# A 32x64 split of the DFT in a fused convolution and MLP kernel: row tiles, column tiles, larger transposes and a new order of work

## The chip, the cores and the metric

The kernel runs on one core of a Trainium2 chip. The metric is the device time of one execution in microseconds (us), less being better. The kernel before took 305.59 us, the median of three runs (304.36 to 305.82). A run is in the "fast" or the "slow" state ("slow" here: over 1.5% above the fastest run of the same kernel), or "unknown" when the kernel ran only once. Verdicts below use fast runs.

Names of engines: PE is TensorE (matrix multiplications), PEld its weight loads, DVE is VectorE, ACT is ScalarE, POOL is GpSimd, SP is SyncE, which here issues all the DMAs. "SPq" is SyncE's queue of instructions. An eviction is the copy of a matmul result out of PSUM, the memory that TensorE writes to. "kv" is the product of the filtered k and v; w1 to w4 are the weight matrices of the MLP (mlp1 is the product with w1); "gin" is what step 4 reads.

## The reference, cut to what matters

```python
def reference(A_q, A_k, A_v, A_shift_k, A_ssm_k, A_ssm_D, B_x, B_w1, ..., gate_w):
    # S = 2048 positions, D = 640 channels, F = 1536
    x = A_q
    g = sigmoid((x * gate_w).sum(-1, keepdims=True))
    # a: 4-tap causal filter of k, times v, then a causal convolution of length S
    kv = causal_filter(A_k, A_shift_k) * A_v
    y  = irfft(rfft(kv, 2*S) * rfft(A_ssm_k, 2*S))[:S] + kv * A_ssm_D
    a  = x * y
    # b: an MLP whose first half shifts four channel groups along the sequence by 1, -1, 2, -2
    h  = gelu(layernorm(x) @ w1)
    x1 = x + shifted(h) @ w2
    b  = x1 + gelu(layernorm(x1) @ w3) @ w4
    return g * a + (1 - g) * b
```

(The long convolution and the shift are condensed here into named helpers.) In both kernels the Fourier transform of length 4096 is done by matrix multiplications: step 1 transforms over the part of the position that lies on the 128 partitions, step 2 over the rest, then comes the product with the transformed filter, and steps 3 and 4 go back. Between the steps the data pass through DRAM.

The parts that the change and the argument touch:

```python
# position s = 16*t2 + t1: partition t2 (128 of them), t1 along the free dimension
q_rows = A_q.rearrange("b (t2 t1) d -> (b t2) t1 d", t1=NT)      # k_rows, v_rows, o_rows alike

def load_x(c):                                   # x is A_q; 4 of these, 640 KB each
    SP.dma_start(out=X[:, 4*c:4*c+4, :], in_=q_rows[:, 4*c:4*c+4, :])

def kv_load(c):
    ...
    SP.dma_start(out=K[:, r:r+n, :], in_=k_src(0, P, t0, n))      # outermost dimension: 128 rows
    SP.dma_start(out=st["KV"][...], in_=v_rows[:, KC*c:KC*c+KC, :])

def step1(name, hf, c, scr, ev):                 # whole array, 128 rows by 128 columns, two halves hf
    ...
            PE.matmul(ps[:, b*512:(b+1)*512], lhsT=F1[:, hf*P:(hf+1)*P], rhs=src[:, o:o+512], ...)
    ...                                          # all evictions of steps 1, 2 and 3 on ScalarE

def h_dma(c):                                    # five small DMA transposes for each quarter of h
    for f in range(4):
        SP.dma_start_transpose(out=st["HT"][:, f, 4*c:4*c+4, HPAD:HPAD+P], in_=hr[:, f]...)
    SP.dma_start_transpose(out=st["HM0"][...], in_=hr[:, 4]...)

def step4(t1, last):                             # two matmuls accumulate into the same 128 rows
    ...
    if t1 % 2 == 0:
        SP.dma_start(out=st["q2"][:], in_=q_rows[:, t1:t1+2, :])
    ...
        SP.dma_start(out=o_rows[:, t1, :], in_=ot[:])
```

## Time and profile before

| | before |
|---|---|
| time, median (range, runs) | 305.59 us (304.36 to 305.82, 3) |
| profiled span, mean granted TensorE clock | 302.3 us, 0.941 |
| busy: PE, DVE, ACT, POOL | 242.2, 176.9, 179.1, 28.3 us |
| last step-3 matmul | 255.7 us |

The first view is part 2 of the page of the kernel before: the span in 40 slices of 7.6 us. Each digit of PE and DMA is the busy share in tenths (DMA: mean over the core's 16 DMA engines), PEclk is the clock granted to TensorE, and the last row is the rate of the DMAs.

```profile
PE   2058858364639888999999999999999999995585
PEclk9999998975968999999999999999999999999559
DMA  6999979585699299958975458554975021775511
GB/s 201 242 259 401 206 202 314 96 236 170 157 283 400 59 269 280 359 205 225 321 288 173 129 193 194 183 173 128 413 242 174 3 87 43 245 278 175 175 43 43
```

TensorE has gaps in the first third and is full after that until the tail. The DMAs are busy in the first third, at 200 to 400 GB/s.

The second view is the kernel before cut into five stretches: for each one its length, then the busy us (and instructions) of PE, PEld, DVE, ACT and POOL, the granted clock, the DMA share and the rate in GB/s.

```profile
core 0: us, PE busy (x) PEld busy (x) DVE busy (x) ACT busy (x) POOL busy (x), PEclk, DMA share, GB/s
0.00:18.40 18.40, 2.83 (x10) 1.37 (x11) 14.13 (x68) 11.44 (x23) 4.56 (x11) 1.00 0.88 223
18.40:66.00 47.60, 34.94 (x240) 19.94 (x240) 37.08 (x89) 33.15 (x68) 5.78 (x4) 0.93 0.91 249
66.00:120.00 54.00, 36.01 (x200) 17.03 (x200) 44.03 (x97) 28.44 (x51) 3.53 (x3) 0.87 0.77 228
120.00:256.00 136.00, 134.04 (x796) 66.04 (x796) 49.59 (x42) 101.44 (x141) 14.45 (x13) 1.00 0.59 196
256.00:302.30 46.30, 34.34 (x191) 16.83 (x189) 32.02 (x50) 4.67 (x6) 0.00 (x0) 0.84 0.48 163
```

From 120 to 256 us TensorE works 134 of 136 us: that stretch is bound by it. The DMA share of the first two stretches is 0.88 and 0.91, so the DMAs are nearly full there too. (Later this view prints shares slightly above 1; read that as full.)

The third view is part 6 of the page, the DMA issues that the change renames: how many, KB of each, and the median us from issue to landing.

```profile
X<-in_A_q_dram SPq DMA_DIRECT2D x4, 640.0 KB, 7.4
KV<-in_A_v_dram SPq DMA_DIRECT2D x8, 320.0 KB, 4.5
q<-in_A_q_dram SPq DMA_DIRECT2D x8, 320.0 KB, 3.1
out_dram<-ot SPq DMA_DIRECT2D x16, 160.0 KB, 1.8
```

On SyncE's queue in the kernel before, the 20 transposes of h (16 to HT, 4 to HM0) take a median of 1.26 us each, and the first starts at 32.9 us.

### The profile page before, as it was taken

Reading aid. Unit: us, or ns where it says so; the run is one execution under the profiler, and the core shown is the slowest. Engines: PE = TensorE matmul, PEld = TensorE weight load, DVE = VectorE, ACT = ScalarE, POOL = GpSimd, SP = SyncE. Lnnn points to the kernel's source line nnn. Section 1 sums busy time; section 2 is a strip of 40 time slices with the busy share of each in tenths; the row PEclk is TensorE's granted clock in tenths of the full one; section 3 lists DMA queues with packets and bytes.
Section 4 is the critical chain, followed back from the end, with each engine's and each line's share of the span. In section 5 each row is a group of like instructions: output and inputs, shape, how many; then the busy total and the mean of one; then the engine's idle time right before and its main releaser. Section 6 shows DMA issues by size and latency. Waiting matters only on the chain.

```text
span 302.3 us, 3944 instructions
## 1 busy us (share of the span) xinstructions
PE 242.2 (80%) x1434; PEld 121.2 (40%) x1434; DVE 176.9 (58%) x344; ACT 179.1 (59%) x284; POOL 28.3 (9%) x31
## 2 busy tenths in 40 slices
PE   2058858364639888999999999999999999995585
PEld 1024535231205444444454445444445454453232
DVE  8767969927899876501125234462343724099983
ACT  1999867242626666997868886469793676400000
POOL 6011302000000211990000000000000000000000
PEclk9999998975968999999999999999999999999559
DMA  6999979585699299958975458554975021775511
GB/s 201 242 259 401 206 202 314 96 236 170 157 283 400 59 269 280 359 205 225 321 288 173 129 193 194 183 173 128 413 242 174 3 87 43 245 278 175 175 43 43
DMA packets 60307, 62.50 MB, mean 207 GB/s; under 512 B 34304, under 2 KB 51457, under 8 KB 60288
## 3 DMA queue, kind: packets, MB, share of 16 engines
q1 hardware_dynamic: 60288, 62.25, 67.2%
q8 instruction: 11, 0.18, 0.2%
q14 instruction: 8, 0.07, 0.1%
HBM read 35.55 MB, written 18.35 MB: 178 GB/s over the span
## 4 chain that ended last, share of the span: by engine, by line
PE 30%; DVE 22%; ACT 13%; SPq 7%; DMA 7%; issue 6%; POOL 1%; ACTq 0%; DVEq 0%; POOLq 0%
PE ps L604 9%; PE ps L596 8%; ACT xs L348 6%; SPq L516 5%; PE ps L321 3%; DVE hs L359 3%; DVE p L358 3%; DVE p L357 3%; PE ps L370 3%; DVE X L558 3%; ACT gs L374 3%; DVE ot L625 2%; ACT stg L323 2%; PE ps L372 2%; PE ps L346 2%
## 5 line engine op out<-in xcount | busy, mean ns | idle before, releaser
L604 PE MATMUL ps<-W,gt 128*128 128x512 bf16 (+1 forms) x384 | 62.5, 306 | 0.8 <-DVE ot L607 0.8
L596 PE MATMUL ps<-x1t,W 128*128 128x512 bf16 x240 | 59.0, 379 | 0.0
L323 ACT CAST stg<-ps 128x1024 bf16<-128x1024 f32 x40 | 38.4, 1020 | 20.5 <-PE ps L321 10.4
L509 PE MATMUL psm<-WA,xt 128*128 128x512 bf16 (+1 forms) x160 | 30.0, 348 | 20.3 <-DVE WA L455 10.2
L604 PEld LDWEIGHTS <-gt 128*128 128x128 bf16 x384 | 30.2, 99 | 24.8 <-issue 3.7
L610 DVE TENSOR_TENSOR X<-ps,X 128x640 bf16<-128x640 f32 x12 | 9.9, 823 | 47.9 <-PE ps L604 47.9
L596 PEld LDWEIGHTS <-W 128*128 128x128 bf16 x240 | 22.3, 97 | 25.2
L357 DVE TENSOR_TENSOR p<-xs,hs 64x2560 bf16<-64x2560 bf16 x8 | 11.9, 1487 | 33.2 <-ACT xs L348 33.2
L374 ACT CAST gs<-ps 128x640 bf16<-128x640 f32 x32 | 20.6, 695 | 16.7 <-PE ps L372 14.5
L597 ACT ACTIVATE gt<-ps 128x1024 bf16<-128x1024 f32 x24 | 24.6, 1027 | 8.0 <-PE ps L596 7.7
L509 PEld LDWEIGHTS <-xt 128*128 128x128 bf16 x160 | 14.9, 111 | 32.0 <-issue 18.5
L346 PE MATMUL ps<-ax,TB 128*128 128x512 bf16 (+1 forms) x128 | 26.2, 298 | 0.3
L554 PE MATMUL psw<-WA,HT 128*128 128x512 bf16 (+1 forms) x128 | 22.4, 306 | 4.6 <-DVE X L558 3.6
L348 ACT CAST xs<-ps 128x640 bf16<-128x640 f32 x32 | 20.2, 696 | 9.0 <-PE ps L346 8.9
L321 PE MATMUL ps<-HT,F 128*128 128x512 bf16 x40 | 13.4, 441 | 13.9 <-ACT stg L323 7.2
L348 ACT CAST hs<-ps 128x640 bf16<-128x640 f32 x32 | 20.3, 696 | 0.1
L464 POOL TENSOR_TENSOR rs<-ve,EXPO 128x4 f32<-128x4 f32 x8 | 10.3, 1290 | 106.7 <-DVE ve L572 70.3
L437 DVE TENSOR_TENSOR acc<-acc,tmp 128x1280 bf16<-128x1280 bf16 x24 | 19.7, 823 | 0.5
L432 DVE TENSOR_TENSOR tmp<-K,cj 128x1280 bf16<-128x1280 bf16 (+1 forms) x25 | 19.8, 794 | 0.4
L510 ACT ACTIVATE hr<-psm,rs 128x640 bf16<-128x640 f32 x16 | 12.6, 807 | 12.4 <-DMA HM<-hr 5.9
L616 PE MATMUL ps<-gin,F 128*128 128x512 bf16 (+1 forms) x64 | 13.4, 347 | 7.4 <-DVE gq L622 6.7
L622 DVE TENSOR_TENSOR gq<-ps,gq 128x640 bf16<-128x640 f32 x16 | 12.6, 825 | 11.0 <-PE ps L616 11.0
(99 smaller groups left out, 309.0 us busy)
## 6 DMA issues: line engine op xcount, KB each, us to landing
S_h<-stg SPq DMA_DIRECT2D x10, 512.0 KB, 4.1
ax<-S_h SPq DMA_DIRECT2D x8, 640.0 KB, 4.2
S_x<-stg SPq DMA_DIRECT2D x10, 512.0 KB, 3.0
ax<-S_x SPq DMA_DIRECT2D x8, 640.0 KB, 4.7
S_g<-gs SPq DMA_DIRECT2D x16, 320.0 KB, 2.3
gin<-S_g SPq DMA_DIRECT2D x8, 640.0 KB, 7.8
W<-in_B_w_dram SPq DMA_DIRECT2D x2, 1920.0 KB, 9.3
X<-in_A_q_dram SPq DMA_DIRECT2D x4, 640.0 KB, 7.4
```

The costliest lines, as they stand in the source:

```text
L321: PE.matmul(ps[:, b * 512:(b + 1) * 512], lhsT=F1[:, hf * P:(hf + 1) * P], rhs=src[:, o:o + 512], start=True, stop=True)
L323: A.copy(out=stg[:, u * 1024:(u + 1) * 1024], in_=ps[:])
L346: PE.matmul(ps[:, o:o + w], lhsT=st["T2"][:, g, :], rhs=ax[:, i, o:o + w], start=True, stop=True)
L348: A.copy(out=dst[:, i, :], in_=ps[:])
L357: V.tensor_tensor(out=p2[0:64], in0=x[0:64], in1=h[64:128], op=ALU.mult)
L374: A.copy(out=gs[:, i % 2, :], in_=ps[:])
L432: V.tensor_tensor(out=dst[:, i:i + n, :], in0=K[:, r:r + n, :], in1=cj[:, j:j + 1, :].to_broadcast([P, n, D]), op=ALU.mult)
L509: PE.matmul(ps[:, o:o + w], lhsT=xt[:, i, k, :], rhs=W1X[:, k, o:o + w], start=(k == 0), stop=(k == DC - 1))
L554: PE.matmul(ps[:, o:o + w], lhsT=h_tile(f, t1), rhs=W2P[:, f, o:o + w], start=(f == 0), stop=(f == 4))
L596: PE.matmul(ps[:, u, :].rearrange("p (a b) -> p a b", a=4), lhsT=st["W3"][:, k, f * P:(f + 1) * P], rhs=xt[:, :, k, :], start=(k == 0), st ...
L597: A.activation(out=gt[:, 2 * (fp % 2):2 * (fp % 2) + 2, :], in_=ps[:], func=ACT.Gelu_apprx_tanh)
L604: PE.matmul(ps[:, o:o + w], lhsT=st["gt", c, f // 4][:, f % 4, i * P:(i + 1) * P], rhs=st["W4"][:, f, o:o + w], start=(f == 0), stop=(f == ...
```

## The change

The intent: with only 64 positions on each half of the partitions, the step-1 matmul needs 64 rows of the array and the step-4 matmul fills 64 columns, so two can run side by side. The position becomes s = 32*t2 + 16*r + t1, and partition 64*r + t2 holds the pair (r, t2). Beside that, 20 small transposes of h become 4 large ones, the shifts are done by copies, part of the evictions goes from ScalarE to VectorE, scaling goes to GpSimd, and the order of all the work is written out as a fixed list.

```diff
-    q_rows = A_q.rearrange("b (t2 t1) d -> (b t2) t1 d", t1=NT)      # v_rows, o_rows alike
+    q_rows = A_q.rearrange("b (t2 r t1) d -> r (b t2) t1 d", r=2, t1=NT)
     def load_x(c):
-        SP.dma_start(out=X[:, 4 * c:4 * c + 4, :], in_=q_rows[:, 4 * c:4 * c + 4, :])
+        SP.dma_start(out=X[:, 4 * c:4 * c + 4, :], in_=q_rows[:, :, 4 * c:4 * c + 4, :])
     # kv_load: K (v alike)
-            SP.dma_start(out=K[:, r:r + n, :], in_=k_src(0, P, t0, n))
+            SP.dma_start(out=K[:, r:r + n, :], in_=bass.AP(..., ap=[[NT * D, 2], [32 * D, H], [D, n], [1, D]]))
     # step 1: two row tiles
-                PE.matmul(ps[:, b * 512:(b + 1) * 512], lhsT=F1[:, hf * P:(hf + 1) * P], rhs=src[:, o:o + 512], ...)
+                PE.matmul(ps[:, r, :], lhsT=F1[H * r:H * r + H, :], rhs=src[H * r:H * r + H, o:o + 512], ...)
     # step 4: two column tiles
-                PE.matmul(ps[:, o:o + w], lhsT=F4[:, hf, :], rhs=st["gin", hf][...], start=(hf == 0), stop=(hf == 1))
+                PE.matmul(ps[H * r:H * r + H, o:o + w1], lhsT=F4[:], rhs=g[:, r, ...], start=True, stop=True)
     # h: one transpose for each quarter
+        SP.dma_start_transpose(out=st["HT"][:, 4 * c:4 * c + 4]..., in_=hr[:]...)
     # q for the end: four loads through a ring of two buffers shared with other tiles; store of one tile
+        q2 = ring.tile([P, 4, D], BF16, name="q2", tag="row", bufs=2)
+        SP.dma_start(out=q2[:], in_=q_rows[:, :, 4 * c:4 * c + 4, :])
+            SP.dma_start(out=o_rows[:, :, t1, :], in_=X1[:, t1, :])
     # order: a list of names; the letters are the engines of the evictions
+        "... step2.h.0.VAVA scale_x1.2.V w4.2 step2.x.0.VAAV table.2 w3.1.0 step2.h.1.AVVA ... "
     (cut: tables, shifts by copy, gating, the rest of the order)
```

## The prediction

> **What bounds the kernel now.** Busy times by stretch show four regimes. From 0 to 66 us TensorE is busy 38 us; from 66 to 120, 36 of 54; from 120 to 256, 134 of 136 at full clock, so that stretch is TensorE-bound; from 256 to 302, 34 of 46. Only the first 120 us and the tail have slack to give back. In the first, the chain of waits runs from 52 to 82 us mostly over SyncE issuing transposes (20 small ones of h at 1.26 us each, plus four of x at 3.2 to 7.6) and then over the VectorE work for kv and w2. In the tail (timeline) VectorE does 0.82 + 0.89 + 0.39 us per step-4 tile while TensorE waits for it, and then 48 w4 matmuls run alone for 9 us.
>
> **Costed changes.**
> 1. Steps 1 and 4 keep their matmul counts (80 and 64) but pair them on disjoint halves of the array. At the 0.216 us spacing of 512-column matmuls seen here, step 1 takes 17 us and step 4 about 8.6. If pairs overlap, 8.6 and 4.3 us of TensorE go. The Trainium skill, "TensorEngine Tiling (Array Packing)", Key Properties, says tiles work in parallel but a mode switch drains the array; step 1 is interleaved with full-array matmuls, so I count half its gain. The transposes of the SSM kernel double to 160 (0.07 us each here: up to +5 us). Net TensorE: −5 to −8 us; step 4's part is not on the critical path.
> 2. h transposes: 20 become 4 of x's size. SyncE saves about 12 us, plus 10 small DMAs, where it is critical. An earlier w1 preparation (ScalarE copies it before the statistics) starts mlp1 at about 13 instead of 18.4 us. I expect w2 to start near 60 us rather than 80 to 90.
> 3. About half of steps 2 and 3's evictions and 15 of step 1's 40 move from ScalarE to VectorE[...], shifts by copy add 7, step 4 gets cheaper. Summing measured durations, VectorE goes from 177 to about 228 us: it becomes the co-bottleneck. ScalarE falls to about 165.
> 4. Scaling of X, some gating and normalisation go to GpSimd. In the trace, four VectorE normalisations took 3.9 us instead of 1.5 while GpSimd built tables, so I add about 5 to 10 us of such blocking.
>
> **Sum.** VectorE work up to the end of kv is about 125 us with 10 idle: kv ends near 135 to 140 (now 101), so the first third becomes VectorE-bound, but TensorE meanwhile finishes w2, the first two w3 groups and one w4 group. TensorE then has about 93 us until the last step 3 (near 237), then 13 us of w4, then step 4 limited by VectorE at about 0.85 us per tile (16 us), plus 3. Prediction: **268 us**, range 252 to 288 (8 in 10). Faster by over 2%: 0.93; within: 0.05; slower: 0.02.
>
> **What shows it.** TensorE idle before 120 us falls from about 46 to under 30 us; 20-block h transposes occupy SyncE under 5 us each; paired matmuls start within tens of ns of each other, and step 1's spacing per pair is near 0.22, not 0.43; VectorE busy share is 80 to 88%; last step-3 matmul near 237; tail after it about 32 us against 46.
>
> **What would make it wrong.** VectorE blocked by GpSimd much more than 10 us, or in-order evictions stalling TensorE in the middle: 280 and above. Tiled matmuls not overlapping: +10. If the VectorE stages overlap better than I credit and kv ends near 120, 250.

## More of the kernel before

The fourth view is the group of the first MLP's matmuls (mlp1) from part 5 of the page: busy us, mean ns of one, then the idle of TensorE just before them and what ended most of it.

```profile
L509 PE MATMUL psm<-WA,xt 128*128 128x512 bf16 (+1 forms) x160 | 30.0, 348 | 20.3 <-DVE WA L455 10.2
```

## The result, and the profile after

| | before | after |
|---|---|---|
| time, median (range, runs) | 304.98 us (303.87 to 305.82, 4) | 499.14 us (498.13 to 500.21, 4) |
| ratio of fast runs (95% interval) | | 1.637 (1.630 to 1.644) |
| profiled span, clock | 302.3 us, 0.941 | 498.4 us, 0.753 |
| busy: PE, DVE, ACT, POOL | 242.2, 176.9, 179.1, 28.3 us | 261.4, 224.3, 150.9, 56.0 us |

A ratio is the mean time of one kernel's fast runs over that of the other's in the same rounds, so it is not quite the ratio of the medians quoted beside it.

The kernel became 194 us slower. No engine has that much more work: VectorE rose by 47 us, TensorE by 19 and GpSimd by 28, and ScalarE fell by 28. So the time is in waiting. Part 2 of the page of the kernel after (a slice is 12.5 us now):

```profile
PE   1214305049771984609194599299999976001000
PEclk9976557559876896657689699789999995555555
DMA  3311711899722519383975475373573493111111
GB/s 93 86 52 46 153 50 51 59 240 232 199 82 85 141 47 133 89 244 117 147 244 136 184 194 153 134 220 108 167 218 94 125 233 71 50 52 51 51 50 44
```

The DMA row rests on the digit 1, and wherever it does, the rate is 44 to 52 GB/s: in four of the first seven slices, in the fifteenth, and in the last six, 75 us. The digit hides the exact share, so such places are read as stretches (the columns are as in the stretches of before; in the first of them other DMAs run too):

```profile
0.00:24.00 24.00, 5.27 (x15) 2.01 (x16) 8.19 (x54) 2.93 (x5) 2.48 (x9) 1.00 0.38 91
60.00:68.00 8.00, 1.81 (x11) 0.77 (x10) 0.00 (x0) 0.00 (x0) 0.00 (x0) 0.71 0.13 51
...
450.00:470.00 20.00, 1.70 (x12) 0.69 (x8) 0.96 (x3) 1.29 (x2) 0.00 (x0) 0.50 0.13 52
476.00:498.40 22.40, 0.00 (x0) 0.00 (x0) 0.00 (x0) 0.00 (x0) 0.00 (x0) 0.50 0.13 47
```

A share of 0.13 is what 2 engines of 16 give (0.125). The share is a mean and could also be 16 engines that are mostly idle, but the start and duration of the single DMA packets in the trace decide it: from 476 to 498 us exactly two packets are under way 85% of the time, and never more than four; in before, from 20 to 40 us, the commonest number is 16. In the last 22 us no compute engine does anything; the share is still 0.13 and the bytes still move. Two engines are working and everybody waits for them. The rate per engine is not low: 51 GB/s over two engines is 25.5 each, and the best slice of before, 413 GB/s over 16, is 25.8 each. A packet of 1280 B takes a median of 55 ns in the tail of after and 56 in that of before.

The waits of the kernel after (engine and line, what was waited for: us in total, times, longest), VectorE's and then SyncE's own, say whose bytes they are:

```profile
DVE q L649 <- DMA q<-in_A_q_dram: 55.2, 3, 23.3
DVE b L499 <- DMA X<-in_A_q_dram: 45.7, 3, 19.3
...
SPq L478 <- DMA X<-in_A_q_dram: 34.8, 2, 26.8
```

These are the loads of X and of q, both renamed (those of K are waited for as well, 12.0 us). The statistics of X on VectorE (L499) wait 46 us, and SyncE stands 35 us, in two waits, in front of transposes of X, and issues nothing behind them meanwhile.

The group of mlp1's matmuls, as for before:

```profile
L526 PE MATMUL psm<-WA,xt 128*128 128x512 bf16 (+1 forms) x160 | 31.8, 372 | 63.1 <-ACT ZG L528 61.5
```

TensorE stood idle 63 us before these matmuls in place of 20, and the view names a ScalarE copy, of all things, as what ended it. ScalarE's timeline around the first of these idles (24.17 + 3.05 to 41.28 us on TensorE) takes the name one step further back. The lines are start, duration, what, and in brackets the idle before it and what ended that:

```profile
36.49 0.74 ACT L494 ACTIVATE jk<-X 128x640 bf16<-128x640 bf16 x1 [9.50 <-DMA X<-in_A_q_dram]
...
40.39 0.79 ACT L527 ACTIVATE hr<-psm,rs 128x640 bf16<-128x640 f32 x1
41.08 0.15 ACT L528 COPY ZG<-psm 128x1 f32<-128x1 f32 x1
```

On ScalarE the statistics of X (L494) stand ahead of these evictions of mlp1 (L527, L528), and they wait 9.5 us for a load of X; only after the evictions does TensorE go on, at 41.28. The idle of TensorE is again that DMA.

The four large transposes of h now hold SyncE for about 13 us (a median of 3.19 each) in place of 25 (20 times 1.26), as predicted. But the first of them starts at 100.4 us and not at 32.9.

The chain of waits of this page is no help: it accounts for 31% of the span only, 26% of it as "issue". And part 6 prints no landing times for this kernel. The DMA share and the waits are the views that find the cause.

Why two engines? The Trainium skill, "DMA: Bandwidth & Descriptors", section "Why a DMA increments its semaphore by 16 and not by 1", says that a DMA is spread over the largest number of engines up to 16 that divides the slowest non-trivial dimension of both access patterns. The section "Rules for kernel authors" adds that an outermost dimension smaller than 16 confines the whole DMA to at most that many engines. In the change the outermost dimension of X, q, K, v and out in DRAM is r, of size 2. Before, it was 128. The trace agrees with the page: 0.13 of 16 engines, two packets at a time.

The size fits as well. Each of the five tensors is 2048 x 640 x 2 bytes = 2.6 MB, 13.1 MB together; at 51 GB/s that is about 257 us of transfers on two engines (an estimate from the rates above). Not all of it has to be exposed.

### The profile page after: what moved, and what is told of

Its sections match the earlier page's. It is cut to its first block, busy times and chain, and to the rows that moved or that the text cites. A ratio compares the mean times of both kernels' runs of the same rounds, so it can differ in the third digit from the quotient of the medians.

```text
span 498.4 us, 4179 instructions
## 1 busy us (share of the span) xinstructions
PE 261.4 (52%) x1519; PEld 123.9 (25%) x1519; DVE 224.3 (45%) x432; ACT 150.9 (30%) x232; POOL 56.0 (11%) x46
## 5 line engine op out<-in xcount | busy, mean ns | idle before, releaser
L619 PE MATMUL ps<-x1t,W 128*128 128x512 bf16 x240 | 67.6, 418 | 2.4 <-DVE X L581 2.4
L321 ACT CAST stg<-ps 128x1024 bf16<-128x1024 f32 x26 | 25.7, 1015 | 64.1 <-DMA S_h<-stg 38.0
L577 PE MATMUL psw<-WA,HT 128*128 128x512 bf16 (+1 forms) x116 | 27.0, 346 | 10.9 <-DVE X L581 9.0
L649 DVE TENSOR_SCALAR q<-q,GS 128x640 bf16<-128x640 bf16 x12 | 5.2, 465 | 61.0 <-DMA q<-in_A_q_dram 55.2
L323 DVE CAST stg<-ps 128x1024 bf16<-128x1024 f32 x14 | 16.9, 1222 | 34.3 <-PE ps L319 16.8
L619 PEld LDWEIGHTS <-W 128*128 128x128 bf16 x240 | 22.8, 103 | 33.3 <-issue 13.4
L662 ACT CAST y<-ps 128x640 bf16<-128x640 f32 x13 | 8.8, 693 | 68.2 <-DVE X L666 49.4
L499 DVE BATCH_NORM_STATS2 b<-X 128x6 f32<-128x320 bf16 x18 | 8.1, 473 | 45.7 <-DMA X<-in_A_q_dram 45.7
L658 PE MATMUL ps<-gin,F 128*64 128x512 bf16 (+1 forms) x64 | 11.0, 465 | 32.7 <-ACT y L662 27.7
L319 PE MATMUL ps<-KV,F 64*128 64x512 bf16 x40 | 8.5, 465 | 37.2 <-ACT stg L321 25.1
L445 DVE TENSOR_TENSOR tmp<-K,cj 128x1280 bf16<-128x1280 bf16 (+1 forms) x25 | 20.4, 814 | 12.1 <-DMA K<-in_A_k_dram 12.0
L623 POOL TENSOR_SCALAR X<-X,OMG 128x640 bf16<-128x640 bf16 x14 | 18.0, 1296 | 38.9 <-DVE xn L598 38.4
L527 ACT ACTIVATE hr<-psm,rs 128x640 bf16<-128x640 f32 x16 | 12.6, 795 | 31.4 <-DMA HT<-hr 25.5
```

What stands on the lines that cost most here:

```text
L319: PE.matmul(ps[:, r, :], lhsT=F1[H * r:H * r + H, :], rhs=src[H * r:H * r + H, o:o + 512], start=True, stop=True)
L321: A.copy(out=stg[:, :, u * 512:(u + 1) * 512], in_=ps[:])
L323: V.tensor_copy(out=stg[:, :, u * 512:(u + 1) * 512], in_=ps[:])
L445: V.tensor_tensor(out=dst[:, i:i + n, :], in0=K[:, r:r + n, :], in1=cj[:, j:j + 1, :].to_broadcast([P, n, D]), op=ALU.mult)
L527: A.activation(out=st["hr", c][:, i].rearrange("p f n -> p (f n)"), in_=ps[:, 0:D], func=ACT.Gelu_apprx_tanh, scale=st["rs", c][:, i:i + 1])
L577: PE.matmul(ps[:, o:o + w], lhsT=h_tile(f, t1), rhs=W2P[:, f, o:o + w], start=(f == 0), stop=(f == 4))
```

## The experiments

The first theory: the outermost dimension of two costs most of the 194 us. The rivals: VectorE blocked by GpSimd and the new assignment of evictions; the drains between tiled and untiled matmuls, or the low granted clock (0.753); and the new order of work.

Every kernel's result was compared with the reference and passed. Three kernels compute something wrong (said below) and passed too, so this comparison does not notice an error in the convolution part.

### split_all: each renamed DMA issued as two, one for each r

```diff
     def load_x(c):
-        SP.dma_start(out=X[:, 4*c:4*c+4, :], in_=q_rows[:, :, 4*c:4*c+4, :])
+        for r in range(2):
+            SP.dma_start(out=X[H*r:H*r+H, 4*c:4*c+4, :], in_=q_rows[r, :, 4*c:4*c+4, :])
     # the same for K, v, q and out; nothing else differs from the kernel after
```

The outermost dimension is then 64, the bytes are the same, and there are more DMAs.

> The changed kernel, with every load and store that names its rows as two runs of 64 (X, q, K, V, the output) issued as two transfers of 64 partitions each; nothing else. Theory A (these transfers run on two of the 16 DMA engines, as the DMA share of 0.13 and 51 GB/s in the idle stretches suggest, and all waits follow from that): 255 to 290 us, and the DMA share no longer rests at 0.13. Rival B (the new order of work stalls in-order queues by itself): above 420 us. Rival C (the tiled matmuls and the low granted clock of 0.75 are the cause): above 420 us, clock still near 0.75.

Measured, three rounds: 323.95 us (321.37 to 325.24), ratio to before 1.061 (1.055 to 1.067). That is over the 255 to 290 us expected and far below the 420 of the rivals; the granted clock is 0.894. So 175 of the 194 us, 90% of the loss, were the outermost dimension. The other 19 us, and the 56 us between 324 and the predicted 268, have other causes. The stretches of split_all, for the later experiments:

```profile
20.00:67.00 47.00, 31.18 (x224) 18.71 (x228) 32.42 (x96) 30.83 (x63) 3.54 (x3) 0.81 1.02 216
67.00:146.00 79.00, 63.05 (x392) 29.75 (x396) 74.69 (x126) 42.14 (x63) 45.42 (x29) 0.93 0.74 203
146.00:269.00 123.00, 117.99 (x698) 56.76 (x709) 89.44 (x92) 59.88 (x79) 2.30 (x2) 0.99 0.65 194
269.00:322.00 53.00, 22.31 (x152) 11.91 (x151) 21.46 (x42) 9.05 (x14) 3.22 (x3) 0.65 0.64 149
```

The DMAs fill the first (share 1.02), VectorE the second (74.7 of 79 us, up to the end of kv at 146), TensorE the third, and nobody the fourth.

### split_xkv and split_qout: half of that repair each

split_xkv splits only X, K and v; split_qout only q and out.

> Only the loads of X, K and V split; q and the output still as two runs. A: the tail keeps its cost: 16 stores of 160 KB and two q loads of 640 KB at 51 GB/s are about 75 us where I predicted a 32 us tail, so 310 to 350 us, with DMA share near 0.13 in the last 70 us. B and C: above 420.

> Only q and the output split; X, K and V still as two runs. A: the first 400 us stay as they are less some 20 us (two q loads lay there), the tail falls to about 35: 410 to 450 us. B and C: within 15 us of 499.

Measured, one look each, beside 304.93 us for before: 396.08 and 430.30 us (state unknown for single runs). The second lies in its expected range; the first is 46 us above its own, which had been built on the predicted tail of 32 us. From the kernel after, the repair of X, K and v alone gives 103 us back and that of q and out alone 69; together that is 172, against 175 for both at once. The two halves act at different ends of the kernel and add up. In split_xkv the whole tail is two-engine traffic, as a stretch of 60 us shows:

```profile
330.00:390.00 60.00, 2.02 (x12) 0.86 (x11) 10.20 (x21) 2.67 (x4) 2.94 (x3) 0.50 0.13 51
```

### before_rows and before_rows4: the same naming put into the kernel before

The converse. The kernel before is left as it is, but the rows of its five tensors are named as two runs of 64 (before_rows) or four runs of 32 (before_rows4). The rows land on other partitions than the tables expect, so both are wrong.

```diff
-    q_rows = A_q.rearrange("b (t2 t1) d -> (b t2) t1 d", t1=NT)
+    q_rows = A_q.rearrange("b (t2 r t1) d -> r (b t2) t1 d", r=2, t1=NT)     # before_rows4: r=4
     # v_rows, o_rows and the source of K alike
```

> The kernel before, its order of work and tiling untouched, with the same five tensors named as two runs of 64 rows (result wrong on purpose: rows of the convolution are permuted). A: 13 MB at 51 GB/s is about 255 us of transfers on two engines, partly hidden: 400 to 520 us. B and C: 300 to 315 us.

> before_rows with four runs of 32 rows in place of two of 64 (result wrong on purpose). If the count of runs in the outer step sets the number of engines: four engines, so the resting DMA share rises from 0.13 to 0.25 and the rate from 51 to about 100 GB/s, and of the 202 us that before_rows lost some 20 to 100 remain: 325 to 405 us. If it is the order of the rows in memory that costs: still near 507.

Measured, one look each: 507.04 us with two runs, beside 304.93 for before, and 391.99 us with four, beside 306.31. The naming alone, without tiles, GpSimd work, transposes or the new order, costs 202 us. With four it costs 86. A stretch of the tail of each:

```profile
462.00:490.00 28.00, 6.16 (x20) 2.73 (x21) 9.57 (x16) 0.00 (x0) 0.00 (x0) 0.50 0.13 50
```

```profile
341.00:380.00 39.00, 18.10 (x71) 8.50 (x72) 24.87 (x39) 0.00 (x0) 0.00 (x0) 0.56 0.25 92
```

The first fence is before_rows: 0.13 of the engines. The second is before_rows4: 0.25, that is 4 of 16, at nearly twice the rate. (Packets under way: two for 90% of the first stretch, four for 75% of the second.) The low clock comes with the naming too: before_rows has none of the tiles and shows 0.773. The share follows the outermost dimension, and the cost follows the share. With this the first theory stands from both sides: taken away, put in, and in two doses.

### What holds the repaired kernel back: qpre, ev_act, no_pool, s1full

Four single changes to split_all, run on one chip beside 304.61 us for before, three rounds each. split_all itself ran earlier, beside 304.93.

**qpre.** In the tail the last two loads of q stand behind stores on SyncE's queue, since the list has them after the first step-4 tiles. SyncE's queue in split_all (start, duration, what, how many):

```profile
288.99 5.27 SPq L633 DMA_DIRECT2D out_dram<-X  x8
294.30 2.25 SPq L648 DMA_DIRECT2D q<-in_A_q_dram  x2
296.65 9.63 SPq L633 DMA_DIRECT2D out_dram<-X  x12
306.38 1.18 SPq L648 DMA_DIRECT2D q<-in_A_q_dram  x2
307.66 11.86 SPq L633 DMA_DIRECT2D out_dram<-X  x12
```

VectorE waits for them:

```profile
DVE q L653 <- DMA q<-in_A_q_dram: 12.1, 2, 6.4
```

qpre puts these two loads into a buffer that is free by then and issues them ahead of the first store.

```diff
-        q2 = ring.tile([P, 4, D], BF16, name="q2", tag="row", bufs=2)
+        q2 = ring.tile(...) if c < 2 else st["q23"][:, c - 2]        # q23: the buffer of the tables, now free
     # order: load_q.2 and load_q.3 right after the last gin, before step4.3 (gin.1.96.128 moves up with them)
```

> split_all, and the last two q loads (which there are issued after the first and second groups of stores, so that step 4 stands still twice, 6.4 and 5.7 us of VectorE waiting for q) go to the buffer of the step tables, free after step 3, and are issued before the first store. If those waits lie on the critical path of the tail: 10 to 14 us less than split_all (310 to 314). If VectorE's work per step-4 tile or the stores set the tail: within 4 us of split_all.

Measured: 314.56 us (313.42 to 316.25), ratio 1.030 (1.024 to 1.037). That is 9.4 us less than split_all, against the 12.1 us of waiting and just under the 10 to 14 expected. The gin load whose name moved in the list is not what helped: the last gin was issued ahead of the first store already in split_all (276.9 us; 275.5 in qpre).

**ev_act.** All evictions of steps 1, 2 and 3 go back to ScalarE, as in before.

```diff
-   "... step1.KV.1.VV ... step2.h.0.VAVA ... step3.1.AAVV ..."
+   "... step1.KV.1.AA ... step2.h.0.AAAA ... step3.1.AAAA ..."
```

> split_all with every eviction of steps 1, 2 and 3 on ScalarE, as before: about 50 us of work move from VectorE to ScalarE. If the balance is what failed (VectorE works without a break from 80 to 147 us while ScalarE is busy 10 us of each 20): kv ends some 12 us earlier and the time falls by 6 to 15 us. If the split of evictions helped TensorE in the later stage: longer by 3 us or more.

Measured: 306.31 us (305.43 to 308.04), ratio 1.004 (0.997 to 1.010). That is 17.6 us less than split_all, above the 6 to 15 expected. The last kv multiplication ends at 139 us in place of 146, and the last step-3 matmul is at 253.1 in place of 268.9. VectorE's busy time falls from 233.0 to 181.8 us and ScalarE's rises from 150.5 to 186.3: the evictions took 51 us of VectorE's time and take 36 of ScalarE's. In split_all one of 128x1024 takes a mean of 1.22 us on VectorE and 1.02 on ScalarE, one of 128x640 0.82 and 0.69.

**no_pool.** The table expansion and the scaling of X go from GpSimd to ScalarE, the normalisation and the gating from GpSimd to VectorE.

```diff
-            G.tensor_scalar(out=dst, in0=src, scalar1=col(c), ...)          # tables; scale_x1 alike
+            A.activation(out=dst, in_=src, func=ACT.Copy, scale=col(c))
-            (G if ev[i] == "G" else V).tensor_scalar(out=xn[:, i, :], ...)  # gate_q alike
+            V.tensor_scalar(out=xn[:, i, :], ...)
```

> split_all with the scaling of X and the building of the step tables moved from GpSimd to ScalarE, and GpSimd's share of normalisation and gating to VectorE; GpSimd keeps its tiny power operations. If GpSimd blocks VectorE (an addition of 0.82 us takes up to 2.5 us beside the tables): the kv operations go back to about 0.82 us, kv ends about 10 us earlier, total 6 to 12 us less. If blocking costs nothing that counts: within 4 us of split_all.

Measured: 310.65 us (308.36 to 314.27), ratio 1.015 (1.007 to 1.022, from its fast runs; the profiled run was slow). That is 13.3 us less than split_all (13.9 without its slow run), just above the 6 to 12 expected, although ScalarE and VectorE now do GpSimd's work: VectorE's busy time still falls, from 233.0 to 220.1 us. The line of the kv additions, in split_all and then in no_pool (duration in ns: least, median, most):

```profile
L452 DVE TENSOR_TENSOR acc<-acc,tmp x24: 805/824/2476, 36.3 to 142.0; 128x1280 bf16<-128x1280 bf16 x24
```

```profile
L452 DVE TENSOR_TENSOR acc<-acc,tmp x24: 807/822/826, 36.2 to 133.9; 128x1280 bf16<-128x1280 bf16 x24
```

The same instruction takes 0.82 us or up to 2.48 us. The Trainium skill, "SBUF — State Buffer", section "SBUF: two separate sides", says that VectorE and GpSimd share one pair of ports under an exclusive lock held for a whole instruction, and that a VectorE instruction with two SBUF inputs contends for it with a GpSimd instruction that reads SBUF. These additions and the table instructions are of those kinds, and the trace agrees: GpSimd's table instructions take a median of 2.1 us, and with them gone the longest addition is 0.826 us.

**s1full.** Step 1 multiplies the whole array again, with everything else as in split_all. Its output is wrong, which doesn't matter for the time.

```diff
-                PE.matmul(ps[:, r, :], lhsT=F1[H*r:H*r+H, :], rhs=src[H*r:H*r+H, o:o+512], ...)
+                PE.matmul(ps[:, r, :], lhsT=F1[:, :], rhs=src[:, o:o+512], ...)
```

> split_all with step 1 on the full array instead of two row tiles (each matmul contracts all 128 rows, so the result is wrong on purpose; matmul count and sizes are kept). If row tiling saves what I counted (half of 8.6 us) and it counts: 3 to 8 us longer. If the drains of the mode switches eat it or it is off the critical path: within 2 us.

Measured: 321.45 us (321.15 to 324.25), ratio 1.055 (1.048 to 1.062), against 1.061 (1.055 to 1.067): the intervals overlap, so the row tiles gave nothing measurable (the run is even 2.5 us shorter, which neither expectation had). The timelines say why. The lines are start, duration, what and how many; first split_all, then s1full:

```profile
119.59 0.61 PE L621 MATMUL ps<-x1t,W 128*128 128x512 bf16 x2
...
120.18 0.39 PE L320 MATMUL ps<-HT,F 64*128 64x512 bf16 x2
...
120.50 0.82 PE L621 MATMUL ps<-x1t,W 128*128 128x512 bf16 x3
```

```profile
118.53 0.59 PE L621 MATMUL ps<-x1t,W 128*128 128x512 bf16 x2
...
119.01 0.59 PE L320 MATMUL ps<-HT,F 128*128 128x512 bf16 x2
...
119.44 1.24 PE L621 MATMUL ps<-x1t,W 128*128 128x512 bf16 x5
```

Two whole-array matmuls of 512 columns take 0.43 us until the next starts (119.01 to 119.44). A tiled pair does overlap: its group takes 0.39 us, against 0.59 for two whole-array ones, and the next matmul starts 0.32 us after it (120.18 to 120.50). But from the two L621 matmuls in front of the pair to the matmul behind it, both kernels need the same 0.91 us here (119.59 to 120.50; 118.53 to 119.44). Over all places in the traces with two such matmuls, a pair and another matmul (14 and 15) the medians of that time are 0.85 and 0.86 us: the tiled pair starts 0.53 us after the first of the two, the whole-array pair 0.43. What the overlap wins behind the pair is lost in front of it. The Trainium skill, "TensorEngine Tiling (Array Packing)", section "Key Properties", says that switching the tiling mode drains TensorE; the 0.10 us of delay agrees with that, though no run isolates a drain. Step 4's column tiles have no such experiment.

### all3 and two: together

all3 is qpre, ev_act and no_pool at once; two is qpre and ev_act. Three rounds, beside 306.31 us for before.

> split_all with the three repairs together: early q loads, all evictions of steps 1 to 3 on ScalarE, GpSimd's work to ScalarE and VectorE. If the gains (9, 18 and 13 us) are of different stages and add up: 283 to 288 us. If relieving VectorE twice pays once, or ScalarE (about 225 us of work then) becomes the limit: 290 to 300.

> split_all with early q loads and the evictions on ScalarE, GpSimd left as it is. If gains add: 295 to 299 us. If it beats all3, ScalarE is the limit there.

Measured: all3 301.55 us (300.62 to 302.81), ratio 0.986 (0.981 to 0.990). two 297.35 us (297.16 to 297.64), ratio 0.971 (0.968 to 0.974). The two gains of qpre and ev_act add up in full: 9.4 + 17.6 = 27.0 us expected from the single ones, 26.6 found. That of no_pool does not add; on top of the others it costs 4 us. (two lies in its expected 295 to 299; all3 missed both of its ranges, the nearer by 1.6 us.) The stretch from 120 to 140 us in all3 and then in two shows it:

```profile
120.00:140.00 20.00, 16.48 (x94) 7.03 (x94) 11.52 (x17) 20.00 (x19) 0.00 (x0) 0.91 0.80 241
```

```profile
120.00:140.00 20.00, 18.35 (x112) 7.57 (x112) 18.30 (x17) 14.83 (x17) 19.89 (x11) 1.00 1.03 308
```

In all3 ScalarE, which has the evictions back and the tables as well, is busy 20.00 of 20 us, and TensorE does 16.5 us. In two, GpSimd builds the tables, VectorE is slowed by it (an addition still takes up to 2.40 us, and kv ends at 137.4 us against 132.8 in all3), and yet TensorE does 18.4 us. So here the full ScalarE costs more than the lock. What it would bring to avoid the lock without loading ScalarE was not tried.

### h_small: the merged transposes undone

From all3, each large transpose of h is issued as five of four blocks, the size that before had.

```diff
-        SP.dma_start_transpose(out=st["HT"][:, 4*c:4*c+4]..., in_=hr[:]...)
+        for a in range(5):
+            SP.dma_start_transpose(out=(block 4*a to 4*a+4 of the same), in_=(columns 512*a to 512*a+512 of the same))
```

> all3 with each large transpose of h issued as five transposes of four blocks, as in the kernel before. If merging them is worth what I said (some 3 us of SyncE per group of four row groups, 12 in all, on the way to w2): 6 to 12 us longer than all3. If SyncE is no longer on the way there: within 3 us.

Measured: 310.41 us (309.67 to 313.19), ratio to before 1.015 (1.009 to 1.021). Merging the transposes is worth 8.9 us to the finished kernel, of the 12 us of SyncE's time that it takes away.

### pair_store: the better version

In two the last result is ready at 286.43 us, but SyncE needs until 292.99 to issue the stores, as its queue shows:

```profile
271.44 21.55 SPq L633 DMA_DIRECT2D out_dram<-X  x32
```

There are 32 issues, two for each of 16 tiles, because the repair doubled them. pair_store is two with one pair of stores for two neighbouring tiles.

```diff
+            fin.add(t1)
+            a = t1 - t1 % 2
+            if a in fin and a + 1 in fin:
                 for r in range(2):
-                    SP.dma_start(out=o_rows[r, :, t1, :], in_=X1[H*r:H*r+H, t1, :])
+                    SP.dma_start(out=o_rows[r, :, a:a+2, :], in_=X1[H*r:H*r+H, a:a+2, :])
```

> two, with one pair of stores per two step-4 tiles (16 transfers of 64 partitions x 2560 B, instead of 32 of 1280 B). In two the last VectorE result is there at 286.4 us, and SyncE still issues stores until 293 at about 0.6 us each. If SyncE's issuing sets the end: 4 to 7 us less than two (290.5 to 293.5). If the landing of the last bytes does: within 2 us of two, or longer because the first stores leave later.

Measured, five rounds: 293.62 us (291.08 to 295.26, 6 runs), before 305.28 (304.14 to 306.82), ratio 0.960 (0.956 to 0.964). It is 3.7 us below two, just under the 4 to 7 expected. Its interval and that of two do not overlap. In its trace the last store is issued 1.5 us after the last result, in place of 6.6. It is the fastest of all the kernels here, 4.0% faster than before and 41% shorter than the change as given.

## Why the prediction was wrong

The prediction said 268 us and 0.93 for a gain; the kernel took 499.

**The step that failed.** It is in the list "Costed changes". The list has four points: matmul tiles, transposes, evictions, GpSimd. The renaming of the rows of X, q, K, v and out is in none of them, and the sum below it silently takes the DMAs of before as unchanged. "What would make it wrong" names VectorE, evictions and tiles, and no DMA. The sum has the first third VectorE-bound and step 4 limited by VectorE; in the kernel after, VectorE is busy 44.0 of the first 120 us, and the last 75 us go at the rate of two engines. The diff showed that each of five tensors got a new outermost dimension of 2, and the profile of before showed that its DMAs ran at a share of 0.88 to 0.91 in the first 66 us, so there was no slack to lose. In place of "unchanged" the runs showed two engines of 16 and 175 us (split_all), 202 us for the naming alone (before_rows) and 86 us for half of the dose (before_rows4).

**The sizes that were wrong beside that.** Repaired, the kernel is at 324 us, still 56 above 268.

- "VectorE becomes the co-bottleneck": right in kind. The predicted 228 us were 224.3 measured in the kernel after and 233.0 in the repaired one. Wrong in what followed: kv ends at 146 us in split_all, not at 135 to 140, and giving the evictions back to ScalarE alone brings 17.6 us (ev_act). The prediction put the moved work down as one fact and did not ask what the same work would cost on ScalarE, which at 150 us busy had room and does them in less time.
- "About 5 to 10 us of such blocking" by GpSimd: 13.3 us (no_pool), the right mechanism and a little more of it.
- "Tail after it about 32 us": 53 in split_all. Of this the late loads of q were 9.4 us (qpre). In two, the store issues were another 4 or so (pair_store: 297.35 to 293.62).
- "Half of step 1's gain" for the tiles: nothing measurable (s1full). Pairs overlap (they start 3 to 6 ns apart), but with the two whole-array matmuls in front a pair took 0.85 us, against 0.86 without tiles. PE's busy time in two is 242.6 us, that of before 242.2, not 5 to 8 less.

**What was right.** Once the DMAs are repaired, mlp1 starts at 13.4 us (predicted 13, before 18.4) and w2 at 60.0 (predicted 60, before 79.6), and TensorE's idle time before 120 us falls from 46.2 us to 31.5, just short of the predicted "under 30" (all in split_all). The merged transposes save about the 12 us of SyncE's time and 8.9 us of the whole. kv ends at 137.4 us in two, in the predicted range, but only with the evictions back on ScalarE, so that hit is luck. The other gains were behind the two-engine DMAs and could not show in the kernel after.

**What stays open.** Between pair_store (293.6) and 268 lie 26 us that no run takes apart. What the traces say of them is reading, not test. The prediction left TensorE 93 us of work between the end of kv and the last step 3; in two it is busy 108 of the 112 us in that place, so it had done less ahead than was assumed, and the last step 3 is at 251.5 us, not 237. And the tail of two, after that, is 44 us. Its stretches, with the TensorE-bound one as the first line:

```profile
140.00:252.00 112.00, 108.17 (x647) 52.87 (x657) 45.93 (x40) 84.69 (x122) 6.57 (x6) 1.00 0.66 199
252.00:269.00 17.00, 15.21 (x109) 8.54 (x111) 3.54 (x4) 2.10 (x3) 0.00 (x0) 1.00 1.01 230
269.00:287.00 18.00, 8.88 (x63) 4.44 (x57) 16.84 (x37) 8.83 (x13) 3.55 (x3) 0.62 0.73 170
287.00:295.40 8.40, 0.00 (x0) 0.00 (x0) 0.00 (x0) 0.00 (x0) 0.00 (x0) 0.50 0.50 108
```

In the 17 us of the second line TensorE works at w4 while step 4 waits for the last step-3 results to come back through DRAM (DMA share 1.01). Then VectorE is the limit of step 4, 16.8 of 18 us, near the 16 that were predicted (though 16 tiles at the 0.85 us named there make 13.6). The last 8.4 us are stores. Why before_rows loses 202 us and the change only 175 was not separated either.

## What to carry to other kernels

When a change renames the dimensions of a tensor in memory, write down the outermost dimension of every DMA that touches it, before and after, and take the new duration into the sum; a change meant for the matrix engine can be decided there. In a profile, a DMA share that rests on a small fraction of 16 (0.13, 0.25) while engines wait is the mark of it. And before work is moved to an engine, ask what else runs there in the same stretch: the same GpSimd work was worth removing while VectorE was full (13 us) and worth keeping where it was ScalarE that would have had to take it and was full (4 us).

## What the Trainium skill lacked or had wrong

- "DMA: Bandwidth & Descriptors", section "Rules for kernel authors", says of two transfers to disjoint partition halves "Don't bother". Here exactly that split took the kernel from 499.14 to 323.95 us. The same table has the rule on the outermost dimension; the two rows should refer to each other, since the first holds only where the single transfer uses all 16 engines already.
- The same page gives the number of engines, but says nothing of how it looks in a profile: a DMA share of 0.13 at 47 to 52 GB/s for two engines, 0.25 at 92 GB/s for four, and a page whose chain of waits accounts for only 31% of the span.
- "TensorEngine Tiling (Array Packing)" says that a change of mode drains TensorE, but not what it costs: here a tiled pair behind two whole-array matmuls started 0.53 us after the first of them, a whole-array pair 0.43, so alternating in pairs gained nothing (0.85 us against 0.86 for all four).
- "SBUF — State Buffer" has the lock between VectorE and GpSimd, but of what VectorE loses by it only one ratio, without shapes: here a 128x1280 bf16 addition of 0.82 us took up to 2.48 us, and taking GpSimd's work away won 13.3 us while VectorE was full.
- "DMA: Bandwidth & Descriptors" gives the issuing engine's time for one plain DMA on "previous generations" only in cycles, in a table made for trn3. In two, each of the 32 stores held SyncE for a median of 0.59 us, and all of them, with their waits, for 21.55.
